# Seven block products for eight in the second MLP's first product, for two of its five token tiles

## The chip, the cores and the metric

One core of one Trainium2 chip runs the whole program. The metric is the device time of one execution in microseconds (us); it was taken in three runs, and one further execution was recorded by the hardware profiler. Times of single instructions and waits all come from that recorded execution.

## What is computed

The program is attention with a memory term, followed by two MLPs over the same 2304 tokens with 512 features each:

```
x = attention(q, k, v, M_prev, z_prev, beta)      # (2304, 512)
h = x @ w_in;   g = where(h > 0, h, exp(min(h, 0)) - 1);   x1 = g @ w_out      # first MLP, 512 -> 2048 -> 512
h = x1 @ w2_in; g = maximum(0.01 * h, h);                  out = g @ w2_out    # second MLP, the same sizes
```

All inputs are 32-bit floats (weights arrive as 64-bit and are decoded on the chip). The change concerns `h = x1 @ w2_in` of the second MLP alone.

## The kernel before

The kernel holds activations transposed: features on the 128 partitions, tokens along the free axis. The 512 features are four chunks of 128, the 2048 hidden features 16 blocks `f` of 128. TensorE works in a reduced form of 32-bit float (fp32r); to keep the precision, each operand is split into a high part (a cast) and a low part (the value minus its high part), and each product is three matmuls: high by high, low weight by high input, high weight by low input.

Stage three, the second MLP, goes over five token tiles (`wide`): four of 512 tokens and one of 256, called tiles 1 to 5 here; the code counts them from zero (`gi`). In each tile the loop over the 16 blocks makes the first product `h_mm` (line 621: four chunks by three matmuls, 128 hidden features by 512 tokens, into one PSUM bank), then the leaky unit (`leaky`, lines 640 and 641, with `g_split`, lines 243 and 628): ScalarE multiplies by 0.01, VectorE takes the maximum, VectorE casts to the high part `gh`, GpSimd subtracts for the low part `gl`. Two blocks later `emit_o3` makes the second product with that block (`out_mm`, line 919: four groups of 128 tokens, three matmuls of 512 columns each), which is accumulated over all 16 blocks in four PSUM banks (`sc` three times, `po`). Block products alternate between the two banks `pm` and the two banks `tp`.

A tile's input is loaded by `load3` through `load_x` (line 832): SP's queue brings 256 tokens at a time into the staging tile `x`, ScalarE casts them (line 241 through `copy`), GpSimd subtracts (line 840). The split inputs lie in `xw` and `xv`, of which there are two pairs (0 and 1) used in turn, so that the next tile is split while the present one is still read. After a tile's last block VectorE copies the four banks to `st` (line 953) in eight pieces, through two buffers, and SP's queue stores them.

Stage two, the second part of the first MLP, goes over the same five tiles; at each tile's end VectorE adds the tile's output into the staging tiles `y` and `x`, and SP's queue writes them to the scratch tensor `x1s` (line 903). The weights of the second MLP are decoded during stage two and the first tile of stage three (`load_w`).

The order of instructions on each engine is made by the scheduler of the tile framework from the order of the program, priorities and a timeline of its own. Engines take their instructions strictly in the order so made, and SP's queue issues its DMAs in order too: one that waits holds back all behind it.

Of the kernel before, what the change touches and what calls it, by code (L numbers as in the profile page):

```python
# [15 lines left out]
P = 128  # L16
# [3 lines left out]
def _f(ap):  # L20
    return ap.bitcast(F32)
# [3 lines left out]
def kernel(  # L25
# [598 lines left out]
    def g_split(g, w):  # L624
        gh = mtile("gh", NG, F32R)[:, 0:w]
        gl = mtile("gl", NG, F32R)[:, 0:w]
        copy("A" if attending else E_GH, gh, g)
        nc.gpsimd.tensor_tensor(out=gl, in0=g, in1=_f(gh), op=ALU.subtract)  # L628
        return gh, gl

    def elu(ph, w):
        e = mtile("e", EB)[:, 0:w]
        nc.scalar.activation(out=e, in_=ph, func=AF.Relu, scale=-1.0)
        nc.scalar.activation(out=e, in_=e, func=AF.Exp, scale=-1.0)
        nc.vector.scalar_tensor_tensor(out=e, in0=e, scalar=-1.0, in1=ph, op0=ALU.add, op1=ALU.max)  # L635
        return g_split(e, w)

# [193 lines left out]

    def load_x(fetch, t0, n):

        xh, xl = (x[:, :, 0:n] for x in wide_x())
        for o in range(0, n, TN):
            xt = mtile("x", 1, F32, (NKC, TN))
            fetch(xt, t0 + o)
            for c in range(NKC):
                copy(E_XH, xh[:, c, o:o + TN], xt[:, c])
                nc.gpsimd.tensor_tensor(  # L840
                    out=xl[:, c, o:o + TN], in0=xt[:, c], in1=_f(xh)[:, c, o:o + TN], op=ALU.subtract
                )
        return xh, xl

    close_mlp()
# [7 lines left out]

    def load3(t0, n):
        return load_x(lambda xt, t: nc.sync.dma_start(xt, x1_scr[t // TW][:, :, t % TW:t % TW + TN]), t0, n)

    with tc.high_priority(offset=EARLY):
        cur = load2(*wide[0])
    for gi, (t0, w) in enumerate(wide):
# [9 lines left out]

        ys = []  # L870

        def fetch_y():
            ne = NKC * TN // w
            for e in range(NKC // ne):
                yt = mtile("yx"[e], 1, F32, (ne, w))
                for pi, (_, _, pw, tok) in enumerate(parts):
                    lo, hi = max(tok, t0), min(tok + pw, t0 + w)
                    if lo < hi:
                        nc.sync.dma_start(
                            yt[:, :, lo - t0:hi - t0], y_scr[pi][:, ne * e:ne * e + ne, lo - tok:hi - tok]  # L880
                        )
                ys.extend(yt[:, i] for i in range(ne))

        for f in range(NFA, NF):
# [15 lines left out]
        for ec in range(NKC):  # L900
            x1 = ys[ec]
            nc.vector.tensor_tensor(out=x1, in0=pys[ec], in1=x1, op=ALU.add)
            nc.sync.dma_start(x1_scr[gi][:, ec], x1)


    for u in w2:
        u()

    cur = load3(*wide[0])
    for gi, (t0, w) in enumerate(wide):  # L910
# [17 lines left out]

        for f in range(NF):
            ph = h_bank()[:, 0:w]  # L930
            h_mm(ph, wi_tiles[1, f], *cur)
            gs[f] = leaky(ph, w)
            if f > 1:
                emit_o3(f - 2)
        if gi + 1 == len(wide):
# [8 lines left out]
            break  # L944
        emit_o3(NF - 2)
        cur = load3(*wide[gi + 1])
        emit_o3(NF - 1)
        for tb in range(w // P):
# [36 lines left out]
```

## Time and profile before

| what | us |
|---|---|
| three runs | 1069.32, 1069.41, 1070.58 (median 1069.41) |
| profiled execution, its own time | 1069.05 |
| its span, first to last instruction | 1067.2 |
| TensorE busy in the span | 1040.3 |
| VectorE, ScalarE, GpSimd busy | 591.8, 485.2, 531.6 |
| tile 2 to tile 3 of stage three, start to start of the same block | 87.04 (759.56 to 846.60) |

The mean granted clock of TensorE is 0.996 of its full 2.4 GHz. Busy time of TensorE in the profile is the union of matmuls that overlap each other; the distance between the starts of neighbours tells what one costs in a row of many. The time before the first and after the last instruction, 1.85 us here, is in the run's time and not in the span.

### The profile page before, as it was taken

Reading aid. Unit: us, or ns where it says so; the run is one execution under the profiler, and the core shown is the slowest. Engines: PE = TensorE matmul, PEld = TensorE weight load, DVE = VectorE, ACT = ScalarE, POOL = GpSimd, SP = SyncE. Lnnn points to the kernel's source line nnn. Section 1 sums busy time; section 2 is a strip of 40 time slices with the busy share of each in tenths; the row PEclk is TensorE's granted clock in tenths of the full one; section 3 lists DMA queues with packets and bytes.
Section 4 is the critical chain, followed back from the end, with each engine's and each line's share of the span. In section 5 each row is a group of like instructions: output and inputs, shape, how many; then the busy total and the mean of one; then the engine's idle time right before and its main releaser. Section 6 shows DMA issues by size and latency. Waiting matters only on the chain.

```text
span 1067.2 us, 17324 instructions
## 1 busy us (share of the span) xinstructions
PE 1040.3 (97%) x5904; PEld 909.9 (85%) x5904; DVE 591.8 (55%) x1380; ACT 485.2 (45%) x1171; POOL 531.6 (50%) x674
## 2 busy tenths in 40 slices
PE   7998899999999999999999999999999999999998
PEld 4786799989998999977888889888888888888897
DVE  6889987888888746566773324654322221232232
ACT  5999887787878735444442225332211211111111
POOL 7675775677668634464643225855422422322222
PEclk9999999999999999999999999999999999999999
DMA  7754553564456249465672304430200100000010
GB/s 183 195 150 112 160 142 96 139 166 142 115 128 164 90 113 337 147 223 168 227 232 85 119 1 138 158 119 1 80 1 1 60 20 1 8 33 1 1 40 20
DMA packets 150120, 115.05 MB, mean 108 GB/s; under 512 B 80016, under 2 KB 141456, under 8 KB 150032
## 3 DMA queue, kind: packets, MB, share of 16 engines
q1 hardware_dynamic: 149888, 113.68, 36.2%
q8 instruction: 47, 0.77, 0.3%
q14 instruction: 41, 0.34, 0.1%
q10 hardware_dynamic: 144, 0.26, 0.1%
HBM read 78.52 MB, written 31.85 MB: 103 GB/s over the span
## 4 chain that ended last, share of the span: by engine, by line
PE 80%; DVE 7%; DMA 4%; ACT 3%; issue 2%; POOL 2%; SPq 1%; DVEq 0%; POOLq 0%; ACTq 0%
PE pm L621 18%; PE sc L919 14%; PE tp L621 14%; PE sc L649 7%; PE pm L649 5%; PE po L919 4%; PE tp L457 4%; PE po L524 4%; PE pm L524 2%; PE po L649 2%; PE sc L426 2%; PE sc L428 1%; PE sc L429 1%; POOL w L138 1%; DMA wraw<-in_moe_w_in_dram 1%
## 5 line engine op out<-in xcount | busy, mean ns | idle before, releaser
L628 POOL TENSOR_TENSOR gl<-e,gh 128x512 fp32r<-128x512 f32 (+2 forms) x181 | 200.4, 1111 | 371.9 <-DVE gh L243 267.8
L621 PE MATMUL tp<-xw,w 128*128 128x512 f32 (+1 forms) x504 | 144.6, 367 | 1.7 <-DVE e L635 1.7
L621 PE MATMUL pm<-xw,w 128*128 128x512 f32 (+1 forms) x496 | 142.7, 369 | 1.2 <-ACT w L241 1.2
L919 PE MATMUL sc<-w,gh 128*128 128x512 f32 x448 | 135.9, 390 | 0.0
L451 POOL TENSOR_SCALAR pt<-pt,rs,omg 128x128 f32<-128x128 f32 (+4 forms) x160 | 104.1, 660 | 21.2 <-DVE rs L446 17.2
L621 PEld LDWEIGHTS tp<-xw,w 128*128 128x128 f32 x504 | 91.8, 188 | 18.3 <-DVE e L635 2.2
L621 PEld LDWEIGHTS pm<-xw,w 128*128 128x128 f32 x496 | 90.5, 188 | 17.7 <-ACT w L241 1.6
L436 ACT ACTIVATE pt<-pt,mx 128x128 f32<-128x128 f32 (+4 forms) x160 | 93.3, 585 | 23.2 <-DVE mx L431 21.6
L649 PE MATMUL sc<-gh,w 128*128 128x512 f32 (+2 forms) x438 | 103.2, 340 | 0.2 <-DVE gh L243 0.2
L919 PEld LDWEIGHTS sc<-w,gh 128*128 128x128 f32 x448 | 83.2, 188 | 16.5
L621 PE MATMUL tp<-xv,w 128*128 128x512 f32 (+1 forms) x252 | 92.6, 367 | 0.0
L621 PE MATMUL pm<-xv,w 128*128 128x512 f32 (+1 forms) x248 | 91.4, 369 | 0.0
L640 ACT ACTIVATE e<-pm 128x512 f32<-128x512 f32 (+1 forms) x40 | 22.2, 555 | 144.7 <-PE pm L621 141.7
L138 POOL TENSOR_TENSOR w<-wm,w 128x512 fp32r<-128x512 f32 x50 | 65.8, 1337 | 43.4 <-ACT w L241 39.4
L457 PE MATMUL tp<-ident,pt 128*128 128x128 f32 x480 | 82.0, 276 | 3.0 <-DVE al L250 1.5
L641 DVE TENSOR_TENSOR e<-tp,e 128x512 f32<-128x512 f32 (+1 forms) x40 | 25.5, 637 | 106.8 <-ACT e L640 106.8
L919 PE MATMUL sc<-w,gl 128*128 128x512 f32 x224 | 84.3, 389 | 0.0
L649 PEld LDWEIGHTS sc<-gh,w 128*128 128x128 f32 x438 | 74.6, 188 | 9.1 <-DVE gh L243 0.6
L641 DVE TENSOR_TENSOR e<-pm,e 128x512 f32<-128x512 f32 (+1 forms) x40 | 25.5, 637 | 102.1 <-ACT e L640 102.1
L621 PE MATMUL pm<-xh,w 128*128 128x288 f32 x368 | 79.6, 302 | 1.7 <-ACT xh L610 1.6
L243 DVE CAST gh<-e 128x512 fp32r<-128x512 f32 (+2 forms) x146 | 71.0, 490 | 13.5 <-PE po L919 3.0
L640 ACT ACTIVATE e<-tp 128x512 f32<-128x512 f32 (+1 forms) x40 | 22.2, 554 | 117.4 <-PE tp L621 117.4
(162 smaller groups left out, 2447.5 us busy)
## 6 DMA issues: line engine op xcount, KB each, us to landing
wraw<-in_moe_w_in_dram SPq DMA_DIRECT2D x32, 512.0 KB, 3.9
wraw<-in_moe_w_out_dram SPq DMA_DIRECT2D x32, 512.0 KB, 4.8
xh<-xh SPq DMA_DIRECT2D x8, 576.0 KB, 3.3
xl<-xl SPq DMA_DIRECT2D x8, 576.0 KB, 4.0
ys<-st SPq DMA_DIRECT2D x32, 144.0 KB, 2.8
x<-x1s SPq DMA_DIRECT2D x9, 512.0 KB, 3.8
vn<-in_v_dram SPq DMA_DIRECT2D x64, 64.0 KB, 2.4
out_dram<-st SPq DMA_DIRECT2D x32, 128.0 KB, 1.7
```

The costliest lines, as they stand in the source:

```text
L138: nc.gpsimd.tensor_tensor(out=w[:, 1, a], in0=t[:, a], in1=_f(w)[:, 0, a], op=ALU.subtract)
L243: (nc.vector if eng == "V" else nc.gpsimd).tensor_copy(dst, src)
L436: nc.scalar.activation(out=pt[0:m, 0:nk], in_=pt[0:m, 0:nk], func=AF.Exp, scale=-1.0, bias=mx[0:m, last:last + 1], accum_out=self.pd["ss"] ...
L451: nc.gpsimd.tensor_scalar(out=pt, in0=pt, scalar1=rs[0:m, i:i + 1], scalar2=omg[0:m, h:h + 1], op0=ALU.mult, op1=ALU.mult,)
L457: nc.tensor.transpose(dst, self.p[c][:, k0:k0 + kn], ident)
L524: nc.tensor.matmul(po[:, a:b], w, x, start=i == 0, stop=i == len(mms) - 1)
L621: nc.tensor.matmul(ph, wi[:, wj, kc, :], xx[:, kc, :], start=n_mm == 0, stop=n_mm == 11)
L628: nc.gpsimd.tensor_tensor(out=gl, in0=g, in1=_f(gh), op=ALU.subtract)
L640: nc.scalar.mul(t, ph, 0.01)
L641: nc.vector.tensor_tensor(out=t, in0=ph, in1=t, op=ALU.max)
L649: nc.tensor.matmul(py, wo[:, wj, ec * P:(ec + 1) * P], gg, start=opens and f == first and n_mm == 0, stop=closes and f == last and n_mm == 2,)
L919: nc.tensor.matmul(pos[tb], gg[:, tb * P:(tb + 1) * P], wo[:, wj, :], start=f == 0 and n_mm == 0, stop=f == NF - 1 and n_mm == 2,)
```

## The change

In tiles 3 and 4 (`FAST = (2, 3)`) two hidden blocks are taken together with the two halves of the 512 features and the two halves of the 512 tokens. That makes a 2 by 2 block matrix product, which is done with seven block products instead of eight (Winograd's form of Strassen's method). A block product is six matmuls of 256 columns (two chunks by three matmuls); it needs sums of weight blocks (s1 to s4) and sums of input blocks (t1 to t4) beside the plain ones, and VectorE and ScalarE put the results together from the PSUM banks. Three of the seven products use plain inputs and are placed first, four use sums of inputs.

- The sums of the inputs are made in stage two by VectorE in the staging tiles `y` and `x` (`combine`, four subtractions of 128x512 per tile, one tile later, behind the second block's unit) and written to scratch tensors `xt`.
- The sums of the weights are made in tile 2 of stage three behind the leaky units of eight blocks (`STEPS`; `combine_w`: six VectorE additions, one ScalarE cast, two GpSimd subtractions), staged in `xw1` and `xv1` in turn and written to scratch `ws` (1 MB for each pair of blocks). Tiles 3 and 4 load them again through the two `wraw` buffers, two pairs ahead (`load_ws`).
- `load3` loads plain inputs in two pieces through `y` and `x`, splits the second piece's low part on VectorE, and for the fast tiles loads the input sums through the same two staging tiles afterwards. Tiles 3, 4 and 5 all take `xw1` and `xv1` for plain inputs; the fast tiles take `xw0` and `xv0` for the sums.
- The next tile's load is issued three second products ahead of the tile's end, where it was two.
- In the fast tiles the leaky unit is one VectorE instruction from SBUF for two 256-column halves, and ScalarE makes the high part.

```
+    def load3(gi):
+        w = wide[gi][1]
+        xh, xl = (mtile(tag, 1, F32R, (NKC, TW))[:, :, 0:w] for tag in (("xw0", "xv0") if gi == 1 else ("xw1", "xv1")))
...
+        for e in range(2 if gi else 0):
+            st = mtile("yx"[e], 1, F32, (2, w))
+            nc.sync.dma_start(st, x1_scr[gi][:, 2 * e:2 * e + 2])
+            for c in range(2):
+                split_to(xh[:, 2 * e + c], xl[:, 2 * e + c], st[:, c], nc.vector if e else nc.gpsimd)
...
+        for e, tag in enumerate(("xw0", "xv0")):
+            t = mtile(tag, 1, F32R, (NKC, TW)).rearrange("p a n -> p (a n)")
+            t = t.rearrange("p (k l c n) -> p k l c n", k=2, l=2, c=2)
+            st = mtile("yx"[e], 1, F32, (2, 2, TW // 2))
+            nc.sync.dma_start(st, xt_scr[gi][:, 2 * e:2 * e + 2])
+            for k in range(2):
+                split_to(t[:, k, 0], t[:, k, 1], st[:, k], nc.gpsimd)
...
+            if later and f == NFA + 1:
+                behind_elu(later.pop())
...
+        def combine(gi=gi, yts=yts):
+            b = [y[:, :, o:o + TW // 2] for y in yts for o in (0, TW // 2)]
+            for k, o, x, y in ((0, 0, 1, 0), (3, 1, 3, 1), (1, 3, 3, 0), (2, 2, 2, 3)):
+                nc.vector.tensor_tensor(out=b[o], in0=b[x], in1=b[y], op=ALU.subtract)
+                nc.sync.dma_start(xt_scr[gi][:, k], b[o])
...
+    def combine_w(pr):
...
+            nc.vector.tensor_tensor(out=s, in0=w[:, 0], in1=w[:, 1], op=ALU.add)
+        for o, a, b, op in ((3, 2, 3, ALU.add), (2, 0, 2, ALU.subtract), (0, 3, 0, ALU.subtract), (1, 1, 0, ALU.subtract)):
+            nc.vector.tensor_tensor(out=t[:, o], in0=t[:, a], in1=t[:, b], op=op)
+        v = mtile(("xw1", "xv1")[pr % 2], 1, F32R, (NKC, TW)).rearrange("p a n -> p (a n)")
...
+        nc.scalar.copy(v[:, 0], t)
+        for k in (0, 2):
+            nc.gpsimd.tensor_tensor(
+                out=v[:, 1, k:k + 2], in0=t[:, k:k + 2], in1=_f(v)[:, 0, k:k + 2], op=ALU.subtract
+            )
+        nc.sync.dma_start(ws_scr[pr], _f(v))
...
+    STEPS = (0, 1, 3, 5, 7, 9, 11, 13)
...
-        for f in range(NF):
-            ph = h_bank()[:, 0:w]
-            h_mm(ph, wi_tiles[1, f], *cur)
-            gs[f] = leaky(ph, w)
-            if f > 1:
-                emit_o3(f - 2)
...
+        def product(wb, xb):
+            out = h_bank()[:, 0:h]
+            for kc in range(2):
+                for n, (a, b) in enumerate(((0, 0), (1, 0), (0, 1))):
+                    nc.tensor.matmul(out, wb[:, a, kc, :], xb[b][:, kc, :], start=kc == n == 0, stop=kc == 1 and n == 2)
+            return out
...
+                nc.scalar.copy(u, product(a11, b11))
+                add(c0[:, 0], product(a12, b21), u)
+                nc.scalar.copy(c0[:, 1], product(s4, b22))
+                nc.scalar.copy(d, product(s1, t1))
+                add(c0[:, 1], c0[:, 1], d)
+                add(u, product(s2, t2), u)
+                add(c0[:, 1], c0[:, 1], u)
+                rows(2 * pr, c0)
+                if pr:
+                    emit_o3(2 * pr - 2)
+                add(u, product(s3, t3), u)
+                add(d, d, u)
+                add(u, product(a22, t4), u)
+                rows(2 * pr + 1, c1)
+                at_use = uses.index((gi, pr)) + 2
+                if at_use < len(uses):
+                    load_ws(uses[at_use])
...
+            if pr == NPR - 1 and gi + 1 < len(wide):
+                cur = load3(gi + 1)
```

How the order moves. On TensorE, at the end of tile 2 and the start of tile 3, before (L621 is the first product, L919 the second; `w_7594` and `w_7750` are the weights of blocks 0 and 1, `xw_10114` and `xv_10115` tile 3's high and low inputs, `w_9014` the weights of the tile before's block 14):

```order
L621 MATMUL pm<-xw_10114,w_7594 128x512 x2
L621 MATMUL pm<-xv_10115,w_7594 128x512
L621 MATMUL pm<-xw_10114,w_7594 128x512 x2
L621 MATMUL pm<-xv_10115,w_7594 128x512
L621 MATMUL pm<-xw_10114,w_7594 128x512 x2
L621 MATMUL pm<-xv_10115,w_7594 128x512
L919 MATMUL sc<-w_9014,gh 128x512 x6
L919 MATMUL sc<-w_9014,gl 128x512 x3
L919 MATMUL po<-w_9014,gh 128x512 x2
L919 MATMUL po<-w_9014,gl 128x512
```

and now, some rows after the plain products of pair 0 have begun (`xw_10208` and `xv_10209` are the plain inputs in xw1 and xv1, `xw_10222` the sums t1 and t2, `xv_10229` t4 and t3, `wraw` the weight sums, L1004 a block product, `w_7760` and `w_7953` plain weights):

```order
L1004 MATMUL pm<-xw_10208,wraw 128x256 x2
L1004 MATMUL pm<-xv_10209,wraw 128x256
L1004 MATMUL tp<-xw_10222,wraw 128x256 x2
L1004 MATMUL pm<-xw_10222,wraw 128x256 x2
L1004 MATMUL pm<-xv_10229,w_7760 128x256 x6
L1004 MATMUL tp<-xv_10229,wraw 128x256 x6
L1004 MATMUL tp<-xw_10222,wraw 128x256 x4
L1004 MATMUL pm<-xw_10222,wraw 128x256 x4
L1004 MATMUL tp<-xw_10208,w_7953 128x256 x2
```

Where whole blocks followed each other, the products on sums stand now in pieces: two matmuls of t1 and two of t2, then t4 and t3, then the rest of t1 and t2, then pair 1.

On SP's queue at the same place, before (L954 stores the output, L855 loads a tile's input):

```order
L855 DMA x<-x1s_120 128x4x256
L954 DMA out_dram<-st 128x256 x8
L855 DMA x<-x1s_120 128x4x256
L855 DMA x<-x1s_121 128x1024
L954 DMA out_dram<-st 128x256 x24
```

and now (L965 stores weight sums, L871 loads input sums, L861 plain inputs, L973 weight sums, L1082 stores the output; `x1s_130` is tile 4's input):

```order
L965 DMA ws_125<-xw_10063 128x2048
L965 DMA ws_126<-xv_10139 128x2048
L871 DMA x<-xt_117 128x1024
L871 DMA y<-xt_117 128x1024
L1082 DMA out_dram<-st 128x256 x2
L861 DMA x<-x1s_130 128x1024
L1082 DMA out_dram<-st 128x256 x2
L861 DMA y<-x1s_130 128x1024
L973 DMA wraw<-ws_121 128x2048
L1082 DMA out_dram<-st 128x256 x4
```

Ahead of the eight stores of the output stand now the last weight sums and the loads of the input sums, and between the stores the loads of the next tile's inputs and of weight sums.

On TensorE at the start of stage three, before (L649 is the second product of the first MLP, `w_7226` its block 14, the others tile 1's first product):

```order
L621 MATMUL pm<-xw_9026,w_7594 128x512 x2
L621 MATMUL tp<-xw_9026,w_7750 128x512
L649 MATMUL sc<-gh,w_7226 128x256 x6
L649 MATMUL po<-gh,w_7226 128x256 x2
L621 MATMUL tp<-xw_9026,w_7750 128x512
L621 MATMUL pm<-xv_9027,w_7594 128x512
L621 MATMUL pm<-xw_9026,w_7594 128x512 x2
```

and now (L655 and L624 are the same lines as L649 and L621, `w_7236` is block 14):

```order
L655 MATMUL sc<-gh,w_7236 128x256 x6
L655 MATMUL po<-gh,w_7236 128x256 x2
L655 MATMUL sc<-gl,w_7236 128x256 x3
L655 MATMUL po<-gl,w_7236 128x256
L624 MATMUL pm<-xw_9052,w_7604 128x512 x2
L624 MATMUL tp<-xw_9052,w_7760 128x512 x2
L624 MATMUL pm<-xw_9052,w_7953 128x512 x2
L624 MATMUL tp<-xw_9052,w_8109 128x512 x2
```

The whole of block 14's second product has moved ahead of tile 1's first matmuls, and eight of these on high inputs follow each other before the first low input.

## Rows read from the trace of the kernel before

**Rows 1.** The page, part 1: busy us (share of the span) and instructions, by engine.

```profile
PE 1040.3 (97%) x5904; PEld 909.9 (85%) x5904; DVE 591.8 (55%) x1380; ACT 485.2 (45%) x1171; POOL 531.6 (50%) x674
```

**Rows 2.** By stretch: PE, PEld, DVE, ACT, POOL busy us (count), PEclk, DMA share, GB/s.

```profile
800.00:900.00 100.00, 100.00 (x443) 82.84 (x442) 23.33 (x44) 13.34 (x26) 29.96 (x27) 1.00 0.07 22
900.00:1000.00 100.00, 100.00 (x443) 82.84 (x442) 24.01 (x45) 12.60 (x23) 26.10 (x22) 1.00 0.03 11
```

**Rows 3.** TensorE in order of time, tile 3, first product: start us, us.

```profile
860.04 0.62 PE L621 MATMUL pm<-xw,w 128*128 128x512 f32 x2
...
860.72 0.62 PE L621 MATMUL pm<-xw,w 128*128 128x512 f32 x2
```

**Rows 4.** TensorE in order of time, tile 5 (256 wide), first product.

```profile
1019.25 0.40 PE L621 MATMUL tp<-xw,w 128*128 128x256 f32 x2
...
1019.61 0.40 PE L621 MATMUL tp<-xw,w 128*128 128x256 f32 x2
```

**Rows 5.** Weight loads in tile 5, by line and form: busy us, mean ns.

```profile
L621 PEld LDWEIGHTS tp<-xw,w 128*128 128x128 f32 x72 | 11.9, 191 | 0.9
```

**Rows 6.** Groups by line and form, from 680 us on: count | busy us, mean ns.

```profile
L641 DVE TENSOR_TENSOR e<-tp,e 128x512 f32<-128x512 f32 x31 | 21.4, 690 | 94.1 <-ACT e L640 94.1
L641 DVE TENSOR_TENSOR e<-tp,e 128x256 f32<-128x256 f32 x8 | 3.4, 425 | 12.6 <-ACT e L640 12.6
L241 ACT CAST xw<-x 128x256 fp32r<-128x256 f32 x24 | 8.0, 403 | 26.3 <-PE tp L621 13.7 <-DMA x<-x1s 12.6
L241 ACT CAST w<-wm 128x1024 fp32r<-128x1024 f32 x6 | 6.3, 1053 | 15.1 <-DVE wm L132 15.1
L628 POOL TENSOR_TENSOR gl<-e,gh 128x512 fp32r<-128x512 f32 x64 | 84.8, 1325 | 200.7 <-DVE gh L243 200.7
L840 POOL TENSOR_TENSOR xv<-x,xw 128x256 fp32r<-128x256 f32 x24 | 17.4, 755 | 12.0 <-ACT xw L241 12.0
```

**Rows 7.** In order of time at 407 us, and line L691 (min/median/max ns): two engines splitting.

```profile
406.24 0.81 POOL L628 TENSOR_TENSOR gl<-e,gh 128x288 fp32r<-128x288 f32 x1 [0.34 <-DVE gh L243]
408.59 3.80 POOL L614 TENSOR_TENSOR xl<-w,xh 128x288 fp32r<-128x288 f32 x4
407.47 3.41 DVE L691 TENSOR_TENSOR w<-w,w 128x288 f32<-128x288 f32 x4
L691 DVE TENSOR_TENSOR x<-x,y x20: 443/454/1071, 220.2 to 397.9; 128x288 f32<-128x288 f32 x20
```

**Rows 8.** The chain in tile 2: start us, us; first products of blocks 13 and 15.

```profile
822.12 2.72 PE tp L621 x12
...
833.00 2.72 PE tp L621 x12
```

**Rows 9.** One block's leaky unit in tile 3, in order of time: first and last step.

```profile
863.02 0.60 ACT L640 ACTIVATE e<-pm 128x512 f32<-128x512 f32 x1 [6.20 <-PE pm L621]
864.44 0.43 DVE L243 CAST gh<-e 128x512 fp32r<-128x512 f32 x1
```

**Rows 10.** DMA issues after 600 us: count, KB each, median us to landing.

```profile
x<-x1s SPq DMA_DIRECT2D x9, 512.0 KB, 3.8
wraw<-in_moe_w_out_dram SPq DMA_DIRECT2D x6, 512.0 KB, 4.5
x1s<-y SPq DMA_DIRECT2D x2, 256.0 KB, 2.1
```

**Rows 11.** Page, part 6: writes of xl, KB, us; view of xl: all its transfers.

```profile
xl<-xl SPq DMA_DIRECT2D x8, 576.0 KB, 4.0
DMA to landing us min/median/max: 3.1/6.9/9.5
```

**Rows 12.** In order of time, SP's queue, ScalarE and TensorE before tile 1 of stage three.

```profile
648.33 0.52 SPq L855 DMA_DIRECT2D x<-x1s  x1
653.43 1.33 ACT L241 CAST xw<-x 128x256 fp32r<-128x256 f32 x4 [1.32 <-DMA x<-x1s]
666.70 0.63 PE L621 MATMUL pm<-xw,w 128*128 128x512 f32 x2
```

More of the change, by code (lines that the diff above doesn't have):

```diff
@@ L159 @@
     y_scr = [dram.tile([P, NKC, p[2]], F32, name=f"ys{i}") for i, p in enumerate(parts)]
+    NPR = NF // 2
+    FAST = (2, 3)
+    xt_scr = {gi: dram.tile([P, 4, 2, TW // 2], F32, name=f"xt{gi}") for gi in FAST}
+    ws_scr = [dram.tile([P, 2, 4, 2 * P], F32, name=f"ws{i}") for i in range(NPR)]
     x1_scr = [dram.tile([P, NKC, min(TW, NT - t)], F32, name=f"x1s{t}") for t in range(0, NT, TW)]
@@ L852, in load2, with split_to, behind_elu @@
         return [x[:, :, 0:n] for x in xs]
-    def load3(t0, n):
-        return load_x(lambda xt, t: nc.sync.dma_start(xt, x1_scr[t // TW][:, :, t % TW:t % TW + TN]), t0, n)
+    def split_to(hi, lo, src, eng):
+        nc.scalar.copy(hi, src)
+        eng.tensor_tensor(out=lo, in0=src, in1=_f(hi), op=ALU.subtract)
+    def load3(gi):
+        w = wide[gi][1]
+        xh, xl = (mtile(tag, 1, F32R, (NKC, TW))[:, :, 0:w] for tag in (("xw0", "xv0") if gi == 1 else ("xw1", "xv1")))
+        for o in range(0, w if gi == 0 else 0, TN):
+            st = mtile("x", 1, F32, (NKC, TN))
+            nc.sync.dma_start(st, x1_scr[gi][:, :, o:o + TN])
+            for c in range(NKC):
+                split_to(xh[:, c, o:o + TN], xl[:, c, o:o + TN], st[:, c], nc.gpsimd)
+        for e in range(2 if gi else 0):
[3 more added lines that the diff above has]
+                split_to(xh[:, 2 * e + c], xl[:, 2 * e + c], st[:, c], nc.vector if e else nc.gpsimd)
+        if gi not in FAST:
+            return xh, xl, None
+        sums = []
+        for e, tag in enumerate(("xw0", "xv0")):
[5 more added lines that the diff above has]
+                split_to(t[:, k, 0], t[:, k, 1], st[:, k], nc.gpsimd)
+                sums.append((t[:, k, 0], t[:, k, 1]))
+        return xh, xl, sums
+    later = []
+    def behind_elu(unit):
+        with ExitStack() as order:
+            for ins in pools["elu"]:
+                order.enter_context(tc.issue_after(ins))
+            unit()
     with tc.high_priority(offset=EARLY):
@@ L868, in emit_out @@
             del gs[f]
-        ys = []
+        ys, yts = [], []
         def fetch_y():
@@ new lines, in add, with rows @@
+        def add(out, a, b):
+            nc.vector.tensor_tensor(out=out, in0=a, in1=b, op=ALU.add)
+        def rows(f, c):
+            flat = c.rearrange("p a n -> p (a n)")
+            nc.vector.scalar_tensor_tensor(out=flat, in0=flat, scalar=0.01, in1=flat, op0=ALU.mult, op1=ALU.max)
+            gh = mtile("gh", NG, F32R)[:, 0:w]
+            gl = mtile("gl", NG, F32R)[:, 0:w]
+            nc.scalar.copy(gh, flat)
+            nc.gpsimd.tensor_tensor(out=gl, in0=flat, in1=_f(gh), op=ALU.subtract)
+            gs[f] = gh, gl
@@ L944 @@
             break
-        emit_o3(NF - 2)
-        cur = load3(*wide[gi + 1])
-        emit_o3(NF - 1)
+        for f in (NF - 2, NF - 1):
+            emit_o3(f)
         for tb in range(w // P):
```

73 lines of the change are left out of this document (54 added, 19 removed).

## The prediction

> **What bounds the kernel now.** I read the page's busy times first, then the busy times by stretch, then TensorE's own order of time in tiles of both widths, and last the chain and the prices of the instructions that are new. TensorE is busy for 97% of the span [rows 1], and over the second MLP's tiles it has no idle time at all, at full granted clock, while VectorE stands at 23 to 24 of 100 us, ScalarE at 13 and GpSimd at 26 to 30 [rows 2]. So in this stage only two things count: how long TensorE's own list is, and whether a new wait opens a hole in it.
>
> Matmul durations overlap, so the price of a matmul is the distance between starts. Three 512-column matmuls of the first product start 0.68 us after the three before them: 0.2267 us each [rows 3]. In the last tile, which is 256 wide, three start 0.36 us apart: 0.12 us each, every one with weights of its own [rows 4]. Halving the width thus costs 53%, not 50%.
>
> **The change, part by part.** *The products.* A pair of hidden blocks takes 2 x 12 = 24 matmuls of 512 columns before, 24 x 0.2267 = 5.44 us; now 7 x 6 = 42 matmuls of 256 columns, 42 x 0.12 = 5.04 us. That is 0.40 us less per pair, with 8 pairs in each of two tiles 16 x 0.40 = 6.4 us. The second product is untouched. Nothing else leaves TensorE's list, so 6.4 us is also the floor: a gain beyond it is excluded, since the waits that could vanish are zero already [rows 2].
>
> *Work beside it.* Per pair VectorE now has seven additions (0.425 us) and two leaky units (0.69 us), 4.4 us; ScalarE three copies and two casts, some 2.4 us; GpSimd two subtractions, 2.65 us [rows 6]; the pair lasts 5.04 + 24 x 0.2267 = 10.5 us. A PSUM bank comes round after three further products, 3 x 0.72 = 2.2 us, and more where second products lie between. A weight-sum load of 1 MB lies between the ends of a 512 KB load (3.8 us) and of two issued in a row (4.5 us plus half a microsecond of issue) [rows 10]; it is asked for two pairs ahead, 10 us or more. I cost all this at nothing; without its cover each pair would show it, 16 times. The weight sums themselves (tile 2) put 2 x 0.69 + 4 x 0.425 = 3.1 us on VectorE, 1.05 us on ScalarE and 2.65 us on GpSimd behind a leaky unit whose result is wanted two blocks later, 4 x 2.72 = 10.9 us [rows 8]: nothing there either.
>
> *The turn from tile 2 to tile 3* is where I expect a hole. Until now the next tile's inputs went into the other buffer pair; now tile 3's plain inputs take the pair (xw1, xv1) in which the weight sums are staged, and its input sums take the pair that tile 2 is still reading. On the clock of the trace before: block 13 starts at 822.12 [rows 8] and ends at 824.84; its leaky unit is through 1.9 us later [rows 9], 826.7; then the last weight sums: VectorE 3.1, ScalarE 1.05, GpSimd 2.65, so 833.5. Their 1 MB write must land before xv1 is free. No row has it. The transfers of xl, writes of 576 KB (4.0) and reads, land in 3.1 us at the fastest and in 9.5 at the slowest [rows 11]; I take 4.9, two 512 KB transfers in a row [rows 10], because the queue is as empty here as there: 838.4. Now GpSimd and VectorE split the plain inputs at the same time. Where they did that before, GpSimd's four took 3.80 us against 0.81 each alone, 17% more, and VectorE went at GpSimd's pace (3.41 for four, 0.454 alone) [rows 7]. So 2 x 1.325 x 1.17 = 3.1 us: the staging tiles are free at 840.9 (x) and 841.5 (y), and only then does SP issue the loads of the input sums, queued in that order; 3.8 us each [rows 10]: 844.7 and 845.3. ScalarE casts four of 512 columns (0.62 each, an estimate on the line between 0.403 for 256 and 1.053 for 1024 [rows 6]): 845.3 to 847.2. GpSimd's four subtractions follow, 1.325 each from 845.4: the last at 850.7.
>
> TensorE meanwhile: block 15 starts at 833.00 and ends at 835.72 [rows 8]; three second products, 8.16 us, and 18 plain-input matmuls, 2.16 us, cover it until 846.04. The four products on sums would end 2.88 us later, 848.9. Their last four matmuls need that last subtraction: 850.7 + 0.5 = 851.2. **Hole: about 2.2 us.** What is late next: the third product of pair 1 wants a bank that VectorE frees only after add, output copy, add, leaky unit, add (4 x 0.425 + 0.69 = 2.4 us, in order), while TensorE has two products, 1.44 us: another 1.0. Together 3.2 us. The ends: with the write at 3.1 the first part shrinks to 0.4 and the second may be hidden, 0.4 in all; with 9.5 it is 7.8.
>
> *The turn into tile 1.* The input sums of tile 4 put four subtractions (2.8 us) and a write (2.1 us [rows 10]) before the load of tile 1's x, which was issued at 648.33 and first used at 653.43 [rows 12]. With the units between, it goes 4.9 to 6.2 us later: first cast 658.3 to 659.6, its four casts and subtractions (0.36 + 4 x 0.755) 3.4, the second load 3.8 to 5.1. Its first piece is ready at 665.8 to 668.4. TensorE reached it at 666.70 [rows 12]; the new order puts 12 more matmuls ahead, so 668.14. I take 0.5 us, ends 0 and 2.5.
>
> *The turn from tile 3 to tile 4.* The plain inputs are free after the third product of pair 7; until tile 4 begins TensorE still has four products (2.88) and four second products (10.9), 13.8 us, against splits of 2.65, a load of 3.8 and four subtractions of 1.325, 11.8 us in a row, and the sums are wanted 2.2 us after that. Nothing; ends 0 and 1.5.
>
> **Sum.** -6.4 + 3.2 + 0.5 + 0 = -2.7 us against the profiled execution's 1069.05: 1066.35. The median of the runs stands 0.36 above that execution; I carry this over: 1066.7. About 0.2%, 2.1 us, is what a measurement of this kernel can tell from no change, so the line runs at 1067.3 and 1071.5.
>
> **The skill against the trace.** Splits on two engines at once cost 17% on GpSimd in the rows [rows 7], and the sum goes by that. The Trainium skill, SBUF — State Buffer, section Who interferes with whom, says that a VectorE instruction with two SBUF inputs and a GpSimd instruction that reads SBUF exclude each other: whichever comes second waits for the whole of the other. By that rule the turn would be dearer and the sum would come to about -0.5; the trace shows the waiting (VectorE at nearly twice its own time), but not the full sum of both. It is rival 2.
>
> **Rivals.**
> 1. *The covers hold.* The 1 MB write lands near 3.1 us, and the turn costs 0.4. For it: all transfers of this stage are short [rows 10]. Against: five serial steps on four engines after it. 1063.4.
> 2. *The two engines take strict turns.* Then the last weight sums wait for one GpSimd subtraction (1.3 us), and the two splits take 2 x (0.69 + 1.325) = 4.0 instead of 3.1 us: 2.2 us later in all, stalls 5.9, net -0.5. For it: VectorE's nearly doubled time [rows 7]; against: GpSimd's mere 17%. About 1068.9, no change that can be told.
> 3. *Slower: transfers at their long end at the turn to tile 3.* Write, split, load and split are serial there; from 5.3 us more than taken (stalls over 8.5) the kernel loses. With the write at 9.5 [rows 11] and the load at 4.5 the stalls are 3.2 + 4.6 + 0.7 + 0.5 = 9.0: 1072.0. For it: such landings are in the trace; against: they stand in stretches with many transfers in flight, while here the DMA share is 0.03 to 0.07 [rows 2].
> 4. *Weight loads bind.* A weight load takes 191 ns in the last tile [rows 5], more than 120; if loads came one after another, a pair would take 42 x 0.191 = 8.0 us, 2.6 more than now, 41 in all: 1108. Against it stand the starts 0.12 apart with those very loads [rows 4]. The Trainium skill, TensorE: Matmul & The Clock Gate, section The mechanism, says that a load overlaps running matmuls only in another row group; these are full 128-row loads, and here the trace disagrees.
>
> **How the numbers follow.** The forecast has 0.40, rival 1 0.17, rival 2 0.31, rival 3 0.11, rival 4 0.01. Faster: 0.57. Same: 0.31. Slower: 0.12. The range leaves out rivals 3 and 4 and the tails: from rival 1's 1063.4 to 1070.4, where rival 2 has a further 1.5 us for the other two turns. The forecast's own range is 1065.6 to 1067.3 (stalls of 2.4 to 4.0).
>
> **What would show it.** In the profile after: 256-column matmuls of the new product line 0.12 us apart; a tile of the fast kind near 8 x 10.48 = 83.8 us where it was 87.0; TensorE idle at the start of tile 3, ended by GpSimd's subtraction of the sums and then by VectorE, 2 to 4 us together; almost none at the start of tile 4 and within pairs. It would be wrong if holes repeat in every pair, if the starts are further apart than 0.12, or if TensorE stands idle elsewhere, in tile 2 above all.

## The result, and the profile after

Forecast 1066.7 us (1063.4 to 1070.4). Measured: a median of **1078.43 us** over 6 runs (1077.37 to 1079.29), beside 1069.81 us over 6 runs of the kernel before; the ratio is 1.0076 with an interval of 1.0062 to 1.0091. The change makes the kernel about 8 us slower, and that lies outside the range. The profiled execution took 1078.19 us (span 1076.4), 9.1 more than that of before.

The page's busy times, against [rows 1]:

```profile
PE 1039.1 (97%) x6192; PEld 919.6 (85%) x6192; DVE 684.9 (64%) x1524; ACT 514.2 (48%) x1223; POOL 554.0 (51%) x678
```

TensorE has 288 more matmuls and nearly the same busy time, as it should; the span grew by time in which it stands. The busy times by stretch, from the end of stage two to tile 5 (columns as in [rows 2]), say where:

```profile
640.00:680.00 40.00, 39.67 (x277) 37.12 (x276) 19.70 (x32) 15.32 (x32) 23.77 (x24) 1.00 0.44 141
680.00:760.00 80.00, 78.33 (x345) 64.22 (x344) 42.74 (x56) 23.19 (x32) 41.57 (x30) 1.00 0.27 88
760.00:850.00 90.00, 90.00 (x406) 74.81 (x405) 61.76 (x92) 19.14 (x28) 46.72 (x34) 1.00 0.33 130
850.00:940.00 90.00, 83.65 (x512) 74.70 (x511) 43.34 (x80) 24.32 (x51) 30.16 (x24) 0.98 0.43 139
940.00:1025.00 85.00, 85.00 (x531) 76.76 (x530) 43.47 (x82) 20.55 (x46) 25.80 (x21) 1.00 0.28 94
```

Tile 2 (to 850) and tile 4 (940 to 1025) have no hole at all; tile 1 (680 to 760) and the start of tile 3 (850 on) have. What TensorE waited for in all of this, in total us, times, longest:

```profile
PE tp L1004 <- ACT xw L848: 4.5, 1, 4.5
PE pm L624 <- DVE e L647: 1.3, 1, 1.3
PE pm L1004 <- DVE e L1008: 1.1, 1, 1.1
PE tp L1004 <- DVE e L1008: 0.8, 1, 0.8
PE sc L987 <- POOL gl L631: 0.4, 1, 0.4
PE pm L624 <- ACT xw L848: 0.3, 1, 0.3
```

No wait repeats from pair to pair. TensorE's order of time: two neighbouring new products in the steady part, the hole at the start of tile 3 with what follows it, and one second product at the same place of tiles 3 and 4:

```profile
850.12 0.28 PE L1004 MATMUL pm<-xv,wraw 128*128 128x256 f32 x1
854.90 0.80 PE L1004 MATMUL tp<-xw,wraw 128*128 128x256 f32 x2 [4.50 <-ACT xw L848]
...
856.29 1.48 PE L1004 MATMUL pm<-xv,w 128*128 128x256 f32 x6
857.57 1.23 PE L1004 MATMUL tp<-xv,wraw 128*128 128x256 f32 x6
...
859.10 0.64 PE L1004 MATMUL pm<-xw,wraw 128*128 128x256 f32 x4
...
861.81 0.50 PE L1004 MATMUL pm<-xw,w 128*128 128x256 f32 x2 [1.10 <-DVE e L1008]
...
863.54 0.51 PE L1004 MATMUL tp<-xw,wraw 128*128 128x256 f32 x2 [0.75 <-DVE e L1008]
...
872.96 0.40 PE L1004 MATMUL pm<-xw,w 128*128 128x256 f32 x2
873.68 0.40 PE L1004 MATMUL tp<-xw,w 128*128 128x256 f32 x2
...
933.50 0.63 PE L987 MATMUL sc<-w,gh 128*128 128x512 f32 x2
...
1017.80 0.63 PE L987 MATMUL sc<-w,gh 128*128 128x512 f32 x2
```

A product of six matmuls takes 873.68 - 872.96 = 0.72 us, 0.12 each. A fast tile takes 1017.80 - 933.50 = 84.30 us where 87.04 were: 2.74 less, 5.5 for both. Behind the 4.5 us hole six matmuls take 857.57 - 856.29 = 1.28 us instead of 0.72. Windows of 5 us show why (the column before the DMA share is TensorE's granted clock):

```profile
850.00:855.00 5.00, 0.50 (x5) 0.30 (x3) 0.34 (x1) 1.91 (x4) 1.39 (x2) 0.99 0.81 242
855.00:860.00 5.00, 5.00 (x26) 4.52 (x27) 0.84 (x3) 1.29 (x4) 3.59 (x3) 0.67 0.55 161
860.00:865.00 5.00, 3.15 (x21) 2.65 (x21) 4.20 (x10) 0.62 (x1) 1.12 (x1) 1.00 0.91 233
```

After the hole the clock is at its lower level, 1.2 of 2.4 GHz, for part of a window.

**The account.** Where starts are further apart than 0.2267 or 0.12 us per matmul, I add up the excess. Turn into tile 1: 2.5 us in three holes, and 0.3 in the first starts behind them. Start of tile 3: 9.3 us, of which 4.7 are the hole, 1.8 the starts at the low clock, 2.2 the two waits for VectorE, the rest small. Products: -5.5. Together +6.3, or +6.6 with the 0.3. From the first write of the output of stage two's fourth tile (644.30 before, 645.79 now) to the last matmul the changed kernel indeed took 6.7 us more than before. The other 2.4 us of the 9.1 lie outside that: 1.5 before it, all of it before 512 us, where nothing of the change has run yet, and 1.0 behind the last matmul. The ten further profiles below put the first of these anywhere from -0.9 to +1.7, so I draw nothing from it, and leave about 1 us of the medians' difference unexplained.

These parts are what stands in the row of starts, not what each would give back if it went alone. The last four matmuls at the low clock (859.10) read GpSimd's last subtraction of the input sums, which ended at 858.59 (856.07 + 2.52, below). The output copy on VectorE at 860.67, behind which the next bank comes free, waited for a store and not for TensorE. So at full clock TensorE would have waited for most of the 1.8 us; no run changes the clock alone.

**What held the hole at the start of tile 3.** The order of time of VectorE, ScalarE, GpSimd and SP's queue, the rows on the chain:

```profile
831.06 3.48 DVE L955 TENSOR_TENSOR wm<-w 128x512 f32<-128x512 f32 x2
834.57 1.80 DVE L957 TENSOR_TENSOR wm<-wm 128x256 f32<-128x256 f32 x4
...
844.98 3.45 DVE L849 TENSOR_TENSOR xv<-x,xw 128x512 fp32r<-128x512 f32 x2 [2.62 <-DMA ws<-xv]
...
860.67 0.42 DVE L1081 COPY st<-sc 128x256 f32<-128x256 f32 x1 [4.50 <-DMA out_dram<-st]
...
852.92 1.14 ACT L848 CAST xv<-x 128x512 fp32r<-128x512 f32 x2 [12.15 <-DMA x<-xt]
854.23 1.14 ACT L848 CAST xw<-y 128x512 fp32r<-128x512 f32 x2 [0.17 <-DMA y<-xt]
...
830.78 3.21 POOL L631 TENSOR_TENSOR gl<-e,gh 128x512 fp32r<-128x512 f32 x2
838.00 2.82 POOL L962 TENSOR_TENSOR xv<-wm,xv 128x512 fp32r<-128x512 f32 x2 [4.01 <-ACT xv L960]
...
856.07 2.52 POOL L849 TENSOR_TENSOR xw<-y,xw 128x512 fp32r<-128x512 f32 x2
...
840.85 0.32 SPq L965 DMA_DIRECT2D ws<-xv  x1
848.46 0.32 SPq L871 DMA_DIRECT2D x<-xt  x1
848.87 0.38 SPq L871 DMA_DIRECT2D y<-xt  x1
...
856.15 0.33 SPq L861 DMA_DIRECT2D x<-x1s  x1
856.57 0.86 SPq L1082 DMA_DIRECT2D out_dram<-st  x2
```

It is the chain of the prediction: last weight sums, their write (840.85, landed 844.9), splits, loads of the input sums (848.46), casts, matmul at 854.90. VectorE is then held for 4.50 us by an output buffer: the copy before was done at 855.4, SP issues its store only at 856.57, behind a load of tile 4's input, and the store lands 4.1 us later.

### The profile page after: what moved, and what is told of

Same layout as the page of the kernel before. It is cut to its first block, busy times and chain, and to the rows that moved or that the text cites. A ratio compares the mean times of both kernels' runs of the same rounds, so it can differ in the third digit from the quotient of the medians.

```text
span 1076.4 us, 18223 instructions
## 1 busy us (share of the span) xinstructions
PE 1039.1 (97%) x6192; PEld 919.6 (85%) x6192; DVE 684.9 (64%) x1524; ACT 514.2 (48%) x1223; POOL 554.0 (51%) x678
## 4 chain that ended last, share of the span: by engine, by line
PE 75%; DVE 8%; DMA 5%; issue 3%; POOL 3%; ACT 3%; SPq 1%; DVEq 0%; ACTq 0%; POOLq 0%
PE pm L624 13%; PE sc L987 13%; PE tp L624 8%; PE sc L655 7%; PE pm L655 5%; PE po L527 4%; PE tp L460 4%; PE po L987 3%; PE tp L1004 3%; PE pm L1004 3%; PE pm L527 2%; PE po L655 2%; PE sc L429 2%; PE sc L431 2%; PE sc L432 2%
## 5 line engine op out<-in xcount | busy, mean ns | idle before, releaser
L631 POOL TENSOR_TENSOR gl<-e,gh 128x512 fp32r<-128x512 f32 (+2 forms) x149 | 160.4, 1081 | 225.8 <-DVE gh L246 117.9
L624 PE MATMUL tp<-xw,w 128*128 128x512 f32 (+1 forms) x376 | 105.1, 360 | 1.7 <-DVE e L639 1.7
L624 PE MATMUL pm<-xw,w 128*128 128x512 f32 (+1 forms) x368 | 103.4, 362 | 2.8 <-DVE e L647 1.3
L655 PE MATMUL sc<-gh,w 128*128 128x512 f32 (+2 forms) x438 | 103.0, 340 | 0.1
L1016 POOL TENSOR_TENSOR gl<-e,gh 128x512 fp32r<-128x512 f32 x32 | 41.5, 1298 | 110.8 <-ACT gh L1015 95.8
L655 PEld LDWEIGHTS sc<-gh,w 128*128 128x128 f32 x438 | 74.5, 188 | 9.1 <-DVE gh L246 0.6
L624 PE MATMUL pm<-xh,w 128*128 128x288 f32 x368 | 80.1, 304 | 1.6 <-ACT xh L613 1.6
L624 PEld LDWEIGHTS tp<-xw,w 128*128 128x128 f32 x376 | 67.9, 189 | 13.3 <-DVE e L639 2.2
L624 PEld LDWEIGHTS pm<-xw,w 128*128 128x128 f32 x368 | 66.2, 188 | 14.9 <-DVE e L647 1.7
L434 DVE CUSTOM_DVE_ANT_0 pt<-sc,mask 128x128 f32<-128x128 f32 (+4 forms) x160 | 69.5, 445 | 8.4 <-PE sc L432 4.4
L460 PEld LDWEIGHTS tp<-ident,pt 128*128 128x128 f32 x480 | 58.3, 141 | 11.0 <-ACT ah L250 2.6
L624 PE MATMUL tp<-xv,w 128*128 128x512 f32 (+1 forms) x188 | 67.6, 360 | 0.0
L624 PE MATMUL pm<-xv,w 128*128 128x512 f32 (+1 forms) x184 | 66.5, 361 | 0.0
L655 PE MATMUL sc<-gl,w 128*128 128x512 f32 (+2 forms) x219 | 65.9, 340 | 0.0
```

Of the source, the lines that this page charges most:

```text
L434: nc.vector.tensor_tensor_reduce(out=pt[0:m, k0:k0 + n], in0=sc[0:m, 0:n], in1=mk, op0=ALU.add, op1=ALU.min, scale=-0.125, scalar=mx[0:m, ...
L460: nc.tensor.transpose(dst, self.p[c][:, k0:k0 + kn], ident)
L624: nc.tensor.matmul(ph, wi[:, wj, kc, :], xx[:, kc, :], start=n_mm == 0, stop=n_mm == 11)
L631: lo = nc.gpsimd.tensor_tensor(out=gl, in0=g, in1=_f(gh), op=ALU.subtract)
L655: nc.tensor.matmul(py, wo[:, wj, ec * P:(ec + 1) * P], gg, start=opens and f == first and n_mm == 0, stop=closes and f == last and n_mm == 2,)
```

## The experiments

Theory: the loss stands at the two turns, as waits in engines' and queues' lists, and the shorter product is a gain. Rivals: it stands in the input sums alone, or is spread over all tiles by the added work.

**1. Last two weight sums two blocks earlier.**

```
-    STEPS = (0, 1, 3, 5, 7, 9, 11, 13)
+    STEPS = (0, 1, 2, 3, 5, 7, 9, 11)
```

> The last two pairs of weight sums are made behind blocks 9 and 11 of tile 2 instead of 11 and 13; nothing else is changed. Theory (the last weight sums sit in xv1 until 844.9 us, and the split of the plain inputs, the staging tiles and the loads of the input sums stand in a row behind them): the plain inputs are split some 10 us earlier, the sums land before TensorE asks for them, the 4.5 us hole and the stretch at a granted clock of 0.67 behind it go, and of the 2.2 us of waits on VectorE behind them some part: 6.5 to 8.7 us less than the changed kernel, 1069.7 to 1071.9. Rival A (the sums are late because they share the staging tiles with the plain inputs and because xw0 and xv0 come free only with tile 2's last block, whatever the weight sums do): the hole stays over 3 us and the time over 1076. Rival B (the loss is spread over all tiles by the added work on VectorE and the added transfers): the first hole may go, but no more than 5 us come back, since the loss stands elsewhere.

Measured 1078.47 us (ratio 1.0082, 1.0068 to 1.0096): nothing gained; the theory's number is a miss. The rows of that kernel, for VectorE, SP, GpSimd and TensorE:

```profile
829.07 1.29 DVE L955 TENSOR_TENSOR wm<-w 128x512 f32<-128x512 f32 x2 [1.99 <-POOL xw L962]
...
837.23 0.32 SPq L965 DMA_DIRECT2D ws<-xv  x1
...
848.26 1.26 POOL L849 TENSOR_TENSOR xv<-x,xv 128x512 fp32r<-128x512 f32 x1 [3.33 <-ACT xv L848]
849.49 1.27 POOL L631 TENSOR_TENSOR gl<-e,gh 128x512 fp32r<-128x512 f32 x1
...
850.80 1.05 PE L987 MATMUL sc<-w,gl 128*128 128x512 f32 x3 [3.12 <-POOL gl L631]
```

The write went out 3.6 us earlier only, for two blocks of 5.44 each, and 1.7 of the 3.6 are a lead that this run had before (its fourth tile's write in stage two stands at 644.07, in the changed kernel at 645.79). The additions wait until GpSimd has read the one buffer `wm` of the pair before, and a pair takes 8 to 9 us through it. The hole then merely changed its releaser: GpSimd's list now had a subtraction of the late input sums ahead of block 15's low part. Two VectorE additions that take 3.48 us beside GpSimd's leaky subtractions in the changed kernel take 1.29 us here, alone.

**2. Tile 2's input split on GpSimd.**

```
-    ..., nc.vector if e else nc.gpsimd)
+    ..., nc.vector if e and gi != 1 else nc.gpsimd)
```

> The second piece of tile 2's input is split for its low part on GpSimd, as its first piece is, instead of on VectorE; nothing else is changed. Theory (VectorE takes its list in order: the split waits from 674.4 to 680.2 us for a load, and tile 1's first leaky units, which free PSUM banks, stand behind it): TensorE's hole of 1.3 us at 684 us goes, 0.5 to 1.5 us less in all, 1076.9 to 1077.9. Rival (the turn into tile 1 is long because the input sums' writes delay tile 1's own load on SP's queue): no change in the time within 0.4 us, the hole comes back as a wait for another engine.

Measured 1079.07 us (1.0091, 1.0076 to 1.0107); TensorE's wait for VectorE in tile 1 is 1.2 us as before, and its wait for GpSimd there grew from 0.4 to 1.3. My reading fell: VectorE's split was one of several instructions in that place. ScalarE's list in the changed kernel shows what stands ahead of all:

```profile
679.56 1.14 ACT L848 CAST xw<-x 128x512 fp32r<-128x512 f32 x2 [4.04 <-DMA x<-x1s]
680.61 1.14 ACT L127 ACTIVATE wm<-wraw 128x1024 f32<-128x1024 f32 x1
681.65 0.58 ACT L646 ACTIVATE e<-pm 128x512 f32<-128x512 f32 x1
```

The cast of tile 2's input waits 4.04 us for its load, and tile 1's first leaky unit, which frees a PSUM bank, stands two places behind it.

**3. That cast placed later.** Tile 2's casts and splits are ordered behind the unit of tile 1's fifth block.

```
+                    if (gi, f) == (0, 4):
+                        held[0] = pools["elu"] + [pools["mul"]]
...
-                cur = load3(gi + 1)
+                cur = behind(gi, lambda: load3(gi + 1))
```

> Tile 2's input is cast and split behind the leaky unit of tile 1's fifth block; until now ScalarE's list has its first cast ahead of tile 1's first leaky unit. Nothing else is asked for; a few weight decodes change places. Theory (ScalarE takes its list in order: the cast of tile 2's input waits 4.0 us for a load, and behind it stand the weight decode and the first leaky units that free the PSUM banks; that is why splitting on another engine did not help): the hole of 1.2 to 1.3 us at 682 us goes, and the wait of 0.4 to 1.3 us for GpSimd some 15 us later shrinks, 1.3 to 2 us less than the changed kernel's 1078.4: 1076.4 to 1077.1. Rival (the input sums' writes push tile 1's own load back on SP's queue, so tile 1 starts late whatever stands behind): under 0.4 us less, the hole stays or comes back elsewhere.

Measured 1075.19 us (1.0050, 1.0037 to 1.0063), more than the theory asked for. TensorE's waits in that kernel:

```profile
PE tp L1013 <- ACT xw L850: 4.5, 1, 4.5
...
PE pm L624 <- ACT xw L850: 0.2, 1, 0.2
```

Tile 1's wait for VectorE and its wait for GpSimd are gone; only the 0.2 for its own input is left. In the profile the stretch from stage two's last write to the last matmul shrank by 2.55 us.

**4. Tile 2's stores on ScalarE's queue,** and **5. tile 4's loads behind those stores** on SP's.

```
-                nc.sync.dma_start(out[r0:r0 + P, cs], o)
+                (nc.scalar if gi == 1 else nc.sync).dma_start(out[r0:r0 + P, cs], o)
```

> The stores of tile 2's output are issued from ScalarE's queue instead of SP's; nothing else is changed, and the order on TensorE, VectorE and GpSimd stays word for word. Theory (behind the first hole VectorE waits 4.5 us for an output buffer whose store stands in SP's queue behind the load of tile 4's plain input, and the additions that free PSUM banks stand behind that copy): the waits of TensorE for VectorE, 1.1 and 0.75 us, go: 1 to 2.2 us less, 1076.2 to 1077.4; the first hole of 4.5 us and the low clock behind it stay. Rival (VectorE would be late anyway, since its additions wait for products that the 1.2 GHz clock holds up): the waits stay, the time stays within 0.5 us of 1078.4.

```
-                nc.sync.dma_start(out[r0:r0 + P, cs], o)
+                held[gi + 1] = [nc.sync.dma_start(out[r0:r0 + P, cs], o).ins]
...
-                cur = load3(gi + 1)
+                cur = behind(gi, lambda: load3(gi + 1))
```

> The loads of tile 4's plain inputs are put behind the last store of tile 2's output on SP's queue; stores stay on SP. TensorE's and ScalarE's and GpSimd's lists stay as in the changed kernel, VectorE makes two of its output copies earlier. Theory (the loads ahead of the stores in SP's list were what held the stores, and with them VectorE): as with the stores on ScalarE's queue, the waits of TensorE for VectorE of 1.1 us at 861 us go, 1 to 2.4 us less, 1076.0 to 1077.4; the first hole, 4 to 4.5 us, and the low clock behind it stay. Rival (moving the stores helped because two queues issue faster than one): no gain, 1078 to 1079.

Measured 1075.99 us (1.0062, 1.0049 to 1.0074) and 1077.06 us (1.0067, 1.0055 to 1.0079). In both the 1.1 us wait for VectorE's addition is gone and the one of 0.8 stays; in 4 a wait of 0.9 us for an output copy on VectorE stands some 7 us behind. So the loads ahead of the stores were what held VectorE at the first of the two waits. Its next additions now wait 2.8 us (4) and 2.5 us (5) for ScalarE's copy of a product from the stretch at the low clock, which is the mechanism of 4's rival. The size is open: the intervals overlap with that of the changed kernel, and in the profiles the time came back as clock (0.50 in 855 to 860 in both, against 0.67).

**6. All sums made, eight products.** Tiles 3 and 4 compute `h_mm` and `leaky` as before; the sums are made, loaded and split, and read by no product.

```
-            if gi in FAST:
+            if False:
...
```

> All additions, casts, subtractions, writes and loads of the sums stay, but tiles 3 and 4 compute the first product with the plain eight block products as before: the sums are loaded and split and no product reads them. It prices what stands beside TensorE. Theory (the side work costs only at the turn into tile 1 and, through the products on sums, at the turn into tile 3): no hole over 1 us at the start of tile 3, the turn into tile 1 still costs about 2.5 us, so 1071.5 to 1073. Rival B (the added work and transfers cost in all tiles): over 1074, with waits inside the tiles.

Measured 1073.12 us (1.0032, 1.0022 to 1.0042), 0.1 above the theory's range; of the 3.8 us by which the median stands above the kernel before, the profile shows 2.7, at the turn into tile 1. TensorE's waits are tile 1's alone (1.3, 0.3 and 0.2 us); through the start of tile 3, with DMA busy at 0.94 to 1.04, TensorE stands nowhere and its clock is 1.00. Placed as in the changed kernel, the added work by itself costs nothing inside the tiles; rival B falls. The hole comes from products that read sums.

**7. Weight sums without `wm`, and earlier.** They are added up in the low half of their staging buffer; the two buffers alternate, so that pairs overlap.

```
-        m = pools["wst"].tile([P, 2 * DM], I32, tag="wm", bufs=pools["nwm"], name="wm")
-        t = _f(m).rearrange("p (k n) -> p k n", k=4)
+        v = mtile(("xw1", "xv1")[pr % 2], 1, F32R, (NKC, TW)).rearrange("p a n -> p (a n)")
+        v = v.rearrange("p (l k n) -> p l k n", l=2, k=4)
+        t = _f(v)[:, 1]
...
+    STEPS = (0, 1, 2, 3, 5, 6, 7, 9)
```

> The weight sums are added up in the low half of their own staging buffer instead of the one shared buffer wm, so that a pair need not wait for the pair before to be split, and are put behind blocks 0, 1, 2, 3, 5, 6, 7 and 9. Theory (moving the last two pairs alone gained nothing because one pair took 8 to 9 us through wm and the last write was 3.6 us earlier only; the hole at the start of tile 3 hangs on that write): the last write of weight sums is issued before 826 us, the input sums are loaded before tile 2's last block ends, TensorE's first hole at the start of tile 3 is under 1 us, the granted clock stays above 0.95 there, 5 to 8.5 us less than 1078.4: 1069.9 to 1073.4, the rest being the turn into tile 1 and VectorE's waits for output buffers. Rival A (xw0 and xv0 come free too late and casts and subtractions after them take too long): hole of 2 us or more, low clock behind it, over 1075. Rival C (more additions at once slow the leaky units of tile 2): new waits inside tile 2, over 1075.

Measured **1069.37 us** (1.0000, 0.9990 to 1.0009): 9 us back by the medians and 8 by the ratios; the theory asked for 5 to 8.5. SP's queue, and two windows of that kernel:

```profile
825.70 0.32 SPq L964 DMA_DIRECT2D ws<-xv  x1
832.02 0.32 SPq L871 DMA_DIRECT2D x<-xt  x1
```

```profile
850.00:855.00 5.00, 5.00 (x39) 4.80 (x39) 3.90 (x10) 1.07 (x3) 0.00 (x0) 1.00 0.39 84
855.00:860.00 5.00, 5.00 (x35) 4.56 (x34) 3.42 (x8) 1.64 (x4) 2.59 (x2) 1.00 0.66 256
```

The last write leaves 15 us earlier, the first load of input sums 16 us earlier (13 and 15, counted from the fourth tile's write of stage two in each kernel), and at the start of tile 3 TensorE has no hole, no low clock, and no wait for VectorE, although the loads still stand ahead of the stores in SP's list: their staging tiles are free early. Rival C's waits did come, 1.4 us for GpSimd inside tile 2, but not its price. The edit changes the buffer and the places together, and no run parts the two.

**8. The three edits together** (3, 5 and 7).

> The three edits together: weight sums without wm and earlier, tile 2's input behind tile 1's fifth block, tile 4's loads behind tile 2's stores. Theory (the loss is the two turns alone; without them the shorter product remains, 5.4 us in the profile of the changed kernel, 8 pairs of 10.54 us in a tile where 87.0 were): 1064.0 to 1067.5, under the kernel before. Rival B (part of the loss is spread over all tiles): 1069 or more although the holes at both turns are gone. Rival A as above: over 1072 with a hole left at the start of tile 3.

Measured **1068.13 us** (0.9980, 0.9970 to 0.9989): faster than the kernel before, though 0.6 over the theory's bracket. Its stretches and waits:

```profile
680.00:760.00 80.00, 80.00 (x355) 66.24 (x354) 41.57 (x53) 21.93 (x29) 41.21 (x30) 1.00 0.26 87
760.00:850.00 90.00, 88.70 (x403) 73.27 (x402) 60.54 (x91) 22.63 (x35) 53.26 (x38) 1.00 0.35 138
850.00:940.00 90.00, 90.00 (x572) 81.69 (x571) 49.57 (x92) 24.47 (x53) 30.55 (x24) 1.00 0.44 149
```

```profile
PE sc L995 <- POOL gl L631: 1.3, 2, 0.9
PE pm L624 <- ACT xw L850: 0.3, 1, 0.3
```

Both turns are clean but for 0.3 us. A smaller cost, which came with 7, stands in tile 2: 1.3 us of waits for GpSimd, where two pairs of weight sums follow each other closely. So of the 5.5 us that the products save, 2.8 are left in the profile between the same two points as in the account, and 1.3 by the medians.

**9. The same with the sums spread out.**

```
-    STEPS = (0, 1, 2, 3, 5, 6, 7, 9)
+    STEPS = (0, 1, 3, 4, 6, 7, 9, 10)
```

> As the kernel with all three edits, with the weight sums behind blocks 0, 1, 3, 4, 6, 7, 9 and 10 instead of 0, 1, 2, 3, 5, 6, 7 and 9. Theory (the waits left in tile 2, 0.87 and 0.42 us for GpSimd, come from two pairs of sums in a row whose subtractions stand before a leaky unit's; the start of tile 3 has some 4 us to spare): one of the two waits goes, no hole at the start of tile 3, 0.3 to 1.5 us less than the kernel with all three edits (1068.1), 1066.6 to 1067.8. Rival (the sums must end behind block 9, or the chain to tile 3 binds again): a hole at the start of tile 3 with a low granted clock behind it, over 1070.

Measured 1067.18 us (0.9983, 0.9974 to 0.9992). One of the two waits is gone, the other is 1.1 us, and 0.5 us of waits for GpSimd stand at the end of stage two; by the ratios the two kernels can't be told apart. The start of tile 3 holds.

**10. The kernel of 8 with eight products.** As in 6, every sum is made and none is read.

> As the kernel with all three edits, but tiles 3 and 4 compute the plain eight block products; every sum is still made, written, loaded and split, and no product reads one. It prices the seven products alone, with no hole at either turn. Theory (a pair costs 10.54 us in the profile instead of 10.88, 16 pairs; the term on record was 6.4 us, the profile of the changed kernel shows 5.4): 5 to 6.5 us more than the kernel with all three edits (1068.1), 1073.1 to 1074.6. Rival D (the shorter product is worth little, since the additions, copies and loads beside it slow its own pairs, and what the three edits gave was only the removal of holes): under 3 us more, below 1071.

Measured 1074.69 us (1.0056, 1.0038 to 1.0074), 6.6 more than 8 by the medians and 8.1 by the ratios; single runs lie wide apart (1072.3 to 1079.0). In the profiles the last matmul is 6.4 us later, 0.9 of it from longer waits in tile 2 (the excess there grew from 1.6 to 2.5 us): 5.4 us for the seven products, as the changed kernel's tile distance gives. Rival D falls. Between the same two points this kernel takes 3.6 us more than the kernel before, in tile 2 and at tile 1's first product: made this early, the sums are not free.

## Why the prediction was wrong

- **Products, -6.4: right in kind, 0.9 too much.** 0.12 us a matmul held. A pair takes 84.30 / 8 = 10.54 us, not 10.48: with second products between the new ones, the first starts of each run of 512-column matmuls lie up to 0.01 further apart, some 0.02 us for each of the three or four runs of a pair.
- **Work beside it, nothing: right for this kernel.** No wait in tiles 3 and 4 behind the start of tile 3, none in tile 2; experiment 6 shows it apart from the products. With the weight sums placed earlier (7 to 10) tile 2 has 1.1 to 2.0 us of waits.
- **Turn from tile 3 to 4, nothing: right** (940 to 1025 without a hole).
- **Turn into tile 1, +0.5: measured 2.5. A step is missing.** For tile 1's own input, the step I priced, about 0.5 was lost. The rest came from tile 2's: its cast, free to start since it has a buffer pair of its own, stands in ScalarE's list ahead of tile 1's first leaky unit. I had asked who waits for the moved loads, and not what is queued behind the instruction that waits for them. Experiment 3 shows it.
- **Turn from tile 2 to 3, +3.2: measured 9.3. This is the step that decided the sign.** The chain was named rightly; its terms for the additions, the splits, the loads and VectorE's waits were too small, and the clock was in none. The last additions begin as forecast, but for the 4.3 us by which all was late by then (1.5 from before stage three, 2.8 from tile 1).
  - (a) VectorE's six additions took 5.3 us instead of 3.1: the two long ones took 3.48 beside GpSimd's two subtractions of 3.21, and 1.29 alone. That is rival 2's mechanism at more than its price, 2.2 us for 1.3. The rule that I weighed there (the Trainium skill, SBUF — State Buffer, Who interferes with whom: the one that comes second waits for the whole of the other) fits these rows better than the 17% of [rows 7], by which the sum went. Taken in turns, two additions of 1.29 together and two subtractions of 1.27 each (both alone, experiment 1) would need 3.8 us; from the first start to the last end they took 3.76.
  - (b) The write was not the trouble: 4.0 us where I took 4.9, so rival 3's long write did not occur, though its sign did. Behind it VectorE's split, which frees x, ended 3.5 us after the landing instead of 2.5.
  - (c) The two loads, issued 0.4 apart, landed in 4.4 and 5.3 us instead of 3.8 [rows 10]; that is the load time of rival 3.
  - (d) The forecast counts its 2.2 us to the matmuls that need the last subtraction. Counted so, 6.5 were measured: 4.7 for the first hole and 1.8 for the slow starts behind it. The subtraction itself ended at 858.59, 3.6 us behind the forecast's 850.7 plus the 4.3; so most of the 6.5 is the chain. The lower clock, 0.67 in 855 to 860, no step of mine had. The Trainium skill, TensorE: Matmul & The Clock Gate, What's actually happening, says that an idle array falls back to the lower clock; these rows agree. What the clock cost beyond the chain stays open.
  - (e) The waits for VectorE, 1.0 forecast, were 2.2: I counted VectorE's own work, and not that a copy in it would wait for a store behind a load on SP's queue (experiments 4 and 5).
- **The end on the slower side** stood at 7.8 us for this turn and 2.5 for the other; at both ends together the sum would have been +3.9, 2.4 below the +6.3 of the account: 0.9 by the products, and 1.5 by the turn to tile 3. Of the other rivals, 1 (the covers hold) and 4 (weight loads bind) did not occur.
- **Slips in the sums**, none of which bears on the outcome: rival 4's 41 us on top of 1069.4 make 1110, not 1108; rival 1's 1063.4 leaves out the 0.5 of tile 1; stalls of 2.4 to 4.0 give 1065.4 to 1067.0.

The signs that I had named came: 0.12 apart, 84.3 for a fast tile, holes at the start of tile 3 first ended by the input sums' chain and then by VectorE, none that repeats from pair to pair. So did a sign of being wrong: TensorE stood idle inside tile 1, where the forecast had priced its start alone. The releaser of the first hole was the cast, not the subtraction, whose end falls among the slow matmuls.

## What to carry to other kernels

When a change hangs new transfers on buffers that are already in use, write down each engine's and queue's list at the turn and ask of every instruction that may wait what stands behind it: here a cast, an output copy and a load each held up work that was ready. A serial chain through one buffer gains little from asking earlier alone: two blocks of head start moved the last write by 2 to 4 us, while two buffers and earlier places together moved it by 13 to 15 and took back the whole loss of 8 us; with the two lists mended as well the kernel is 1 to 2 us faster than before. And when a hole in TensorE's list is priced, ask what its clock does behind it, and what would hold TensorE there at full clock.

## What was not expected of the hardware

The clock: in all six profiles with a hole of 3.1 to 4.6 us at the start of tile 3 (the changed kernel and experiments 1 to 5) the granted clock in one of the 5 us windows that follow is 0.50 to 0.70, and in the five without it (6 to 10) TensorE runs on unbroken there (in the windows of 6, 7 and 8 at 1.00). In the changed kernel the matmuls behind the hole of 4.7 us took 1.8 us longer, most of it under a wait that would have stood there anyway. VectorE's additions with both inputs in SBUF took 2.7 times as long beside GpSimd's subtractions (3.48 against 1.29 us for two), far from the 17% that GpSimd itself had shown [rows 7]; GpSimd's own two took 3.21 against 2.54 alone. How dear the meeting is depends on which of the two one looks at.
